# A convolution block moved from VectorE to ScalarE and GpSimd, and a swap and a load moved ahead, in the first steps of a fused convolution and GELU MLP

## The chip, the cores and the metric

The kernel runs on 1 core of one Trainium2 chip. Times are device microseconds of one execution of the program. An engine is TensorE (PE; its weight loads are PEld), VectorE (DVE), ScalarE (ACT), GpSimd (POOL) or SyncE (SP, which here only issues DMAs). PSUM is the memory that TensorE writes, SBUF the one that all engines share.

## The reference

x has shape (8, 4096, 192) and goes through two blocks. The first is a causal convolution along the sequence, with 7 taps per head, softmaxed; 8 heads share the 192 channels. The second takes each of the 32768 tokens through two products with a quick GELU between them. All is float32.

```python
w = softmax(weight)                       # (8 heads, 7 taps)
x_pad = concat([zeros(B, 6, D), x], axis=1)
out[b, s, h, g] = sum_k w[h, k] * x_pad[b, s + k, h, g]
h = out.reshape(32768, 192) @ w_in        # (192, 2048)
g = h * (1 / (1 + exp(-1.702 * h)))
y = g @ w_out                             # (2048, 192)
```

## The kernel before, in words

The 32768 tokens are cut into 32 steps. A step (`big` in the code) takes 512 tokens from each of two halves of the batch. Channels lie on partitions; the 192 channels are three chunks `c` of 64, and a chunk's 512 tokens lie as two halves of 256 on the two halves of the partitions. A block of the convolution is named by its number: chunk c, batch half n is block 2c + n.

A step has two parts on TensorE. The first product is `hidden`: w_in times the convolved x. It runs a list written out by hand, `HIDDEN`, of 40 terms and the instructions between them. Each term is one product of a sum of weight blocks with a sum of convolution blocks (a fast matrix multiplication: fewer products, more sums). The sums of weight blocks are `SUMS_W`, made once, in steps 0 and 1. The sums of convolution blocks are made anew in every step (blocks 6 to 19). VectorE joins the products (`join`), ScalarE copies them out of PSUM and computes the GELU into the buffer `g`. The second product is `second`, with a hand-written list `PLAN`: w_out times g, again with sums. The weight forms of this product are `w_form`.

While step s is in these two parts, step s+1's convolution blocks are summed and step s+2's x is transposed and convolved. What step s+1 needs:

- The x of a step is loaded by `load_x` (L87, DMAs at L99, 8 of them on SP's queue) into `xin`, of which there is one buffer, and turned by three transposes on VectorE (`transpose_x`, L518) into `xts`, of which there is one buffer too.
- The taps. From step 3 on, all three chunks are convolved by ScalarE taps (`tap`, L570: one tap times x, into a free half of some block of `g` or `room`) and added by GpSimd, VectorE and accumulating DMAs. For step 2 only chunks 0 and 2 go this way, and the adding is by accumulating DMAs on GpSimd's queue (`end_taps`, L600). They form a tree: for the homes of taps 1 to 6 and the result 0, first (1,2), (3,4), (5,6), then (0,1), (3,5), and (0,3) last. Chunk 1 of step 2 is convolved on VectorE: seven instructions in `conv` (L551 once, L553 six times), from the generator `prepare`.
- The sums of blocks (`sum_of`, L604, printed as L435 and L437 inside `add_up`) and the swap of a block (`cross_run`, L609: two DMAs on SP's queue that bring each half of the partitions to the other, since a term wants both halves on each).

In step 1 the sums and swaps for step 2 are held back until the third `("turn",)` in `HIDDEN`. At that point the list calls `need("done 2")`, which issues the last two accumulating DMAs of chunk 2, and then GpSimd makes two sums for block 12 (`over`, L870) and five others, and SP swaps them as they come. `("fetch",)`, the fourth term from the end of the list's 41 products, is step 2's first term and reads block 12.

Step 0 is written out (`first_step`); its second product is `second_first` (L922), in which `go` runs the products (L980) and pops one entry of the list `side` beside each (L985). At its end, and in step 1's first product, runs everything that is done once: 24 sums of weight blocks on VectorE for one half of w_in and 18 for the other (`sums_w_in`, L445), block 13's sum and swap, the last four forms of w_out (`add_forms(3)`: four ScalarE copies and four accumulating DMAs, L482), the turns and stores of step 0's output (L1091, L1102), and the load of x for step 3. The pieces that go beside the list are in `beside`: from the second join on, each join takes one entry off it (L819).

In the listing, the lines that the change touches are L685 (`prepare`), L818 (`join`), L845 (`turn`), L913 (the end of `hidden`), L1002 to L1074 (`second_first`), and L1078 (`convs_next`).

Of the kernel before, what the change touches and what calls it, by code (L numbers as in the profile page):

```python
# [15 lines left out]
def kernel(  # L16
# [29 lines left out]
    nc = tc.nc  # L46

    B, S, D = x.shape
    H, K = weight.shape
# [5 lines left out]
    NC = D // R  # L55
# [25 lines left out]
    vec, act = nc.vector, nc.scalar  # L81
# [5 lines left out]
    def load_x(big, ns=range(2)):  # L87


        p, c = divmod(big, CHUNKS)  # L90
        if c == 0 and 0 in ns:
            (nc.gpsimd if big else vec).memset(xin[0:R, :, 0, :], 0.0)
        for n in ns:
            for o in range(2):
                j = 1 if c == 0 and o == 0 else 0
                t = c * TOK + o * T + (j - 1) * Q
                for v in range(2):
                    q0 = o * R + v * Q
                    nc.sync.dma_start(  # L99
                        out=xin[q0 : q0 + Q, n, j:NJ, :],  # L100
                        in_=x_v[n, p, t : t + (NJ - j) * Q, v * Q : v * Q + XW].rearrange(
                            "(j i) d -> i j d", i=Q
                        ),
                    )
# [33 lines left out]
    def spot(i):  # L138

        if i >= SPOTS:  # L140
            return block(*divmod(i - SPOTS, NG))
        flat = osbs[:, i * BLK : (i + 1) * BLK] if i < 2 else room[:, ROOMS[i - 2], :]
        return flat.rearrange("p (k t) -> p k t", k=NG)
# [55 lines left out]
    def own(big):  # L199
        return conv_t[:, big % 2 * NR : big % 2 * NR + NR, :]  # L200
# [13 lines left out]
    SUMS_ES = [  # L214
        (13, 0, "-", 3), (14, 1, "-", 3), (15, 1, "-", 11),
    ]
# [228 lines left out]
    def sums_w_in(v, n0=0, n1=None):  # L445
        for item in SUMS_W[v][n0:n1]:
            add_up(lambda j: w_in_s[:, j, v * P : (v + 1) * P], *item)
# [63 lines left out]
    cw = consts.tile([P, NC, K], F32)  # L511
# [31 lines left out]
    def conv_src(big, c, k, ns=slice(0, 2)):  # L543
        return xts[big][:, c, ns, Q - PAD + k : Q - PAD + k + T]
# [57 lines left out]
    def sum_of(big, item, eng=None):  # L602

        add_up(lambda i: pair(big, i)[:, 0, :], *item, eng=eng or nc.gpsimd)  # L604
# [8 lines left out]
    def cross_run(big, b0, b1, eng=None):  # L613

        (o, x), n = places_of(big, b0), b1 - b0
        cross(conv_t[:, x : x + n, :], conv_t[:, o : o + n, :], eng)
# [7 lines left out]
    V_E = (V_F[1], V_F[1] + NV_E)  # L624
# [59 lines left out]

    def prepare(big):  # L685

        if big < 3:
            for k in range(K):
                yield "", 0.76 if k else 0.48, lambda k=k: conv(big, 1, k)
        yield f"conv {big}", 0.0, lambda: None  # L690
        if big == 1:
            dst = own(1)[:, 0:2, :]
            for k in (1, 3, 5):
                yield "", 0.7, lambda k=k: vec.tensor_add(dst, dst, tap_home(1, 0, k))
        yield f"done {big}", 0.0, lambda: (need(f"taps {big}"), end_taps())
# [71 lines left out]
    FETCH, NEXT = (1, 0), (3, 1, 2, 0)  # L767
# [7 lines left out]
    def hidden(big, tiles, work):  # L775
# [34 lines left out]
        def join(dst, a, op, b):  # L810
            flat = "o" not in (dst[0], a[0], b[0])
            if dst[0] == a[0] == b[0] == "k":
                banks = [[KS[int(n[1:])] for n in (dst, a, b)]]
            else:
                banks = [[bank(n, h) if flat else ot(bank(n, h)) for n in (dst, a, b)] for h in range(2)]
            for out, x, y in banks:
                (vec.tensor_add if op == "+" else vec.tensor_sub)(out, x, y)  # L817
            seen_joins.append(0)  # L818
            if beside and len(seen_joins) > 1:  # L819
                beside.pop(0)()  # L820

        def gelu(i, src, sign):
            dst = g_rows(i)
# [13 lines left out]
        def next_turn():  # L837
            c = next(turns)
            if c == 0:
                need(f"done {big + 1}")  # L840
            transpose_x(big + 2, c)
            if c == NC - 1 and big + 3 < N_BIG:
                load_x(big + 3)

        def turn():  # L845
            seen.append(0)
            if big > 1:
                if big + 2 < N_BIG:
                    next_turn()
            elif len(seen) == 1:  # L850
                add_forms(3)
            elif len(seen) == NC:
                while beside:
                    beside.pop(0)()
                next_turn()
                need("forms")
                held.clear()
                while waiting:
                    waiting.pop(0)()
# [52 lines left out]
        )  # L912
        for item in HIDDEN:  # L913
            do[item[0]](*item[1:])
        if big == 1:
            for _ in range(1, NC):
                next_turn()

    def chunk_cols(c):
        return slice(c * Q, (c + 1) * Q)  # L920
# [1 line left out]
    def second_first(between, fetch, last_taps):  # L922
# [40 lines left out]
        def listed(w, t, gs=(0, 1)):  # L963
            return [
                (w[i][:, v, h, :], t[i][:, v, :, h * T : (h + 1) * T])
                for i in gs for v in range(2) for h in range(2)
            ]
# [9 lines left out]
        def go(bank, steps, first=True, more=False):  # L977
            for i, (w, t) in enumerate(steps):
                for c in range(NC):
                    nc.tensor.matmul(  # L980
                        chunk(bank, c), w[:, chunk_cols(c)], t,
                        start=first and i == 0, stop=not more and i == len(steps) - 1, skip_group_check=True,
                    )
                dst, w, t, start, to = side.pop(0)
                nc.tensor.matmul(dst, w, t, start=start, stop=to is not False, skip_group_check=True)  # L985
                if to is not False:
                    act.copy(to, dst)
# [3 lines left out]
        def sums_b(i):  # L991
# [10 lines left out]
        p2, p3 = listed(a12, b21), listed(s4, b22)  # L1002
        aside(
            (sums[0], sums[1], c11),
            (listed(s1, t1, (0,)), None, True), (listed(s1, t1, (1,)), p5, False), (p3[:6], q12, False),
        )
        last_taps()
        add_forms(0)
        sub(t1[1], b12[1], b11[1])
# [24 lines left out]
        act.copy(whole(c21), whole(a))  # L1034
        add(p5, p5, whole(a))
        go(c12, p3[6:], first=False)
        sums_w_in(FETCH[0], 0, 3)
        sums_w_in(1 - FETCH[0], 0, 24)
        next_tap()
# [7 lines left out]
        fetch()  # L1047
        act.copy(last, whole(c21))
        add(q12, q12, whole(c12))
        sum_of(1, SUMS_ES[0], vec)  # L1050
        cross_run(1, V_E[0], V_E[0] + 1)
        sums_w_in(1 - FETCH[0], 24)

        def after_1():
# [7 lines left out]
        def beside_1():  # L1062
            turn(0, 0, blocks(p1), js)
            for item in SUMS_ES[1:]:
                sum_of(1, item, vec)
            cross_run(1, V_E[0] + 1, V_S[1])
            store(0, 0)
            load_x(3)

        after_copy.extend([after_1, after_2])  # L1070
        beside.append(beside_1)
        for i in range(3, len(SUMS_W[FETCH[0]]), 6):
            beside.append(lambda i=i: sums_w_in(FETCH[0], i, i + 6))
        beside.extend([lambda: convs_next(1)] * K)  # L1074

    after_copy, beside = [], []

    def convs_next(n):  # L1078
        for _ in range(n):
            if todo and not todo[0][0]:  # L1080
                todo.pop(0)[2]()

    def blocks(t):
        return t.rearrange("p (j t) -> p j t", t=Q)
# [387 lines left out]
```

## Time and profile before

| | us |
|---|---|
| median of 3 runs | 2269.74 |
| lowest and highest run | 2267.92, 2270.87 |
| the profiled execution | 2267.85 |
| its span (first to last instruction) | 2266.1 |
| PE busy | 2251.1 (99%) |
| DVE busy | 2114.3 (93%) |
| ACT busy | 1710.6 (75%) |
| POOL busy | 985.0 (43%) |

The profile is of one execution. Each row of a timeline gives start and length in us, engine, line, operation, out<-in and shapes, then in brackets the idle time of the engine before it and what ended it. Instructions of one kind in a row are merged, with their count (x8). A group row gives the count, the busy time in us and the mean of one in ns, then the idle time before them. A DMA's row gives the time of its issue; when its data has landed is a number of its own. L12 is line 12 of the kernel.

### The profile page before, as it was taken

The numbers are of one execution on the slowest core, as the hardware profiler recorded it, in microseconds if no ns is written. First come the engines' busy times: TensorE is split into PE (matmuls) and PEld (weight loads), VectorE is DVE, ScalarE is ACT, GpSimd is POOL, SyncE is SP. The second block draws the span as 40 slices with busy tenths as digits, with TensorE's granted clock in tenths as the row PEclk, the third lists the DMA queues.
The fourth block names the chain that finished last, engine by engine and source line by source line (L and its number), as shares of the span: only waits on it lengthen the run. The fifth ranks groups of instructions, "written<-read, shape, count | busy, mean of one in ns | idle before, by whom it ended". The sixth has DMA issues, their size and how long they took to land.

```text
span 2266.1 us, 63896 instructions
## 1 busy us (share of the span) xinstructions
PE 2251.1 (99%) x25090; PEld 1345.5 (59%) x25090; DVE 2114.3 (93%) x3268; ACT 1710.6 (75%) x3335; POOL 985.0 (43%) x1009
## 2 busy tenths in 40 slices
PE   9999999999999999999999999999999999999999
PEld 5356656666556666566665566665666656666555
DVE  8999999999999999999999999999999999999998
ACT  8767777777877777777778777787777877777854
POOL 1534554444543445434445435454344454344510
PEclk9999999999999999999999999999999999999999
DMA  9986778767688767787676886677876768765743
GB/s 204 160 169 141 143 143 168 150 134 146 136 159 164 142 138 143 146 169 145 138 147 134 161 162 140 137 143 148 169 143 138 147 136 165 157 137 112 138 95 71
DMA packets 341995, 329.66 MB, mean 145 GB/s; under 512 B 131648, under 2 KB 280768, under 8 KB 341696
## 3 DMA queue, kind: packets, MB, share of 16 engines
q0 software_dynamic: 66352, 167.47, 41.9%
q1 hardware_dynamic: 273696, 157.72, 30.4%
q8 instruction: 199, 3.26, 0.6%
q14 instruction: 100, 0.82, 0.1%
q10 hardware_dynamic: 1648, 0.39, 0.1%
HBM read 53.15 MB, written 25.17 MB: 35 GB/s over the span
## 4 chain that ended last, share of the span: by engine, by line
PE 96%; issue 1%; DMA 1%; SPq 1%; DVE 1%; ACT 0%; POOL 0%; DVEq 0%; POOLq 0%; ACTq 0%
PE slot L709 37%; PE slot L1172 28%; PE sums L1172 17%; PE sums L709 13%; PE slot L980 2%; DMA xin<-in_x_dram 0%; SPq L99 0%; DMA osbs<-room 0%; SPq L1102 0%; POOL conv_t L437 0%; DVE xt L518 0%; DVE g L435 0%; ACT conv_t L1278 0%; DVE conv_t L437 0%; POOL g L1148 0%
## 5 line engine op out<-in xcount | busy, mean ns | idle before, releaser
L709 PE MATMUL slot<-conv_t,w_in_s 64*128 64x512 f32 x3372 | 823.6, 593 | 3.5 <-ACT slot L802 2.4
L1172 PE MATMUL slot<-g,w_form 128*32 128x256 f32 x5872 | 713.4, 379 | 0.8 <-ACT slot L1201 0.8
L709 PEld LDWEIGHTS slot<-conv_t,w_in_s 64*128 64x128 f32 x3372 | 449.8, 187 | 287.9 <-issue 175.0
L437 DVE TENSOR_TENSOR g<-g 128x1024 f32<-128x1024 f32 x372 | 443.5, 1219 | 10.8 <-ACT g L833 1.9
L1172 PE MATMUL sums<-g,w_form 128*32 128x256 f32 x3800 | 422.2, 379 | 0.0
L1172 PEld LDWEIGHTS slot<-g,w_form 128*32 128x32 f32 x5872 | 364.1, 110 | 90.9 <-ACT slot L1201 1.2
L826 ACT ACTIVATE g<-slot 128x512 f32<-128x512 f32 x494 | 265.1, 625 | 132.0 <-PE slot L709 131.4
L709 PE MATMUL sums<-conv_t,w_in_s 64*128 64x512 f32 x1284 | 346.7, 592 | 0.9 <-DMA conv_t<-conv_t 0.6
L1172 PE MATMUL slot<-g,w_out_s 128*32 128x256 f32 x4080 | 321.4, 379 | 0.9 <-DVE g L437 0.5
L1148 POOL DMA_DIRECT2D g<-g x124 | 116.5, 939 | 450.5 <-PE slot L1172 252.4
L1197 ACT COPY room<-slot 32x256 f32<-32x256 f32 x434 | 158.4, 365 | 186.7 <-PE slot L1172 172.8
L570 ACT ACTIVATE g<-xt,cw 128x512 f32<-128x512 f32 x389 | 270.2, 719 | 4.4
L437 POOL TENSOR_TENSOR conv_t<-conv_t 128x256 f32<-128x256 f32 x210 | 195.4, 948 | 152.4 <-PE slot L709 90.3
L1172 PEld LDWEIGHTS sums<-g,w_form 128*32 128x32 f32 x3800 | 211.0, 110 | 69.6
L1172 PEld LDWEIGHTS slot<-g,w_out_s 128*32 128x32 f32 x4080 | 166.0, 110 | 127.0 <-ACT g L826 11.4
L906 POOL TENSOR_TENSOR conv_t<-conv_t,g 128x512 f32<-128x512 f32 x174 | 238.6, 1393 | 4.5
L709 PEld LDWEIGHTS sums<-conv_t,w_in_s 64*128 64x128 f32 x1284 | 171.1, 187 | 106.2 <-issue 56.2
L833 ACT ACTIVATE g<-g 128x1024 f32<-128x1024 f32 x155 | 170.7, 1101 | 1.5 <-DVE g L817 1.5
L906 POOL TENSOR_TENSOR g<-g 128x512 f32<-128x512 f32 x87 | 110.7, 1273 | 121.9 <-ACT g L570 119.6
L1197 ACT COPY room<-sums 32x256 f32<-32x256 f32 x217 | 79.3, 366 | 104.7 <-PE sums L1172 92.2
L709 PE MATMUL slot<-g,w_in_s 64*128 64x512 f32 x556 | 149.7, 593 | 1.7 <-DVE slot L817 1.7
L826 ACT ACTIVATE g<-sums 128x512 f32<-128x512 f32 x188 | 103.8, 615 | 58.6 <-PE sums L709 58.1
(243 smaller groups left out, 3901.7 us busy)
## 6 DMA issues: line engine op xcount, KB each, us to landing
g<-g POOLq DMA_DIRECT2D x124, 512.0 KB, 6.6
conv_t<-conv_t SPq DMA_DIRECT2D x844, 64.0 KB, 2.0
xin<-in_x_dram SPq DMA_DIRECT2D x240, 180.0 KB, 6.3
out_dram<-osbs SPq DMA_DIRECT2D x186, 128.0 KB, 2.5
g<-g POOLq DMA_DIRECT2D x66, 256.0 KB, 6.5
g<-g SPq DMA_DIRECT2D x248, 64.0 KB, 3.6
g<-room POOLq DMA_DIRECT2D x31, 512.0 KB, 6.1
g<-osbs POOLq DMA_DIRECT2D x30, 512.0 KB, 6.5
```

Of the source, the lines that this page charges most:

```text
L437: eng.tensor_sub(v(dst), v(a), v(b))
L570: act.mul(home, conv_src(big, c, k), cw[:, c, k : k + 1])
L709: nc.tensor.matmul(slot[h], w_in_s[halves[h], a, v * P : (v + 1) * P], src, start=first, stop=True, skip_group_check=True,)
L826: act.activation(dst[:, :, h, :], ot(bank(src, h)), AF.Gelu_apprx_sigmoid, scale=float(sign))
L833: act.activation(dst.rearrange("p o h t -> p h o t"), src, AF.Gelu_apprx_sigmoid, scale=float(sign))
L906: (vec if eng == "v" else nc.gpsimd).tensor_add(dst, dst, home)
L980: nc.tensor.matmul(chunk(bank, c), w[:, chunk_cols(c)], t, start=first and i == 0, stop=not more and i == len(steps) - 1, skip_group_check ...
L1148: nc.gpsimd.dma_start(out=spot(dst), in_=spot(a), accum_op=ALU.add)
L1172: nc.tensor.matmul(dst, w, t, start=first, stop=last, skip_group_check=True)
L1197: act.copy(to, d)
```

## The change

Five things are changed.

- Chunk 1 of step 2 is no longer convolved by VectorE (`prepare` starts at step 2 without it). Its seven taps become ScalarE taps, and six GpSimd adds in their new function `middle_tap`, each add right behind its tap in the program's order. The homes of taps 1 to 6 are halves of spots 11, 12, 15, 3, 3 and 11; taps 1 and 2 lie where the GELU of output block 5 is to be written, tap 3 where that of block 9 is, tap 6 where that of block 7 is.
- The 18 weight sums that remain go two to each of nine joins, with a tap beside each of the first seven; before, they went six to each of three joins, with a convolution instruction to each of the next seven.
- Block 13's sum and swap, and the load of x for step 3, go out in `second_first` before the last 24 weight sums, ahead of step 0's stores on SP's queue. Before, the sum and swap came after the last product of step 0 and the load after the first joins of step 1 and the stores.
- So that the swap can go there, the last 18 entries of `side` are reordered: the steps that read the memory of block 13's swap come first, and the three column chunks alternate.
- Step 3's transposes go out at the twelfth join, the third turn and the thirteenth join; before, one at the third turn and two after the list. With the last of them goes the load of x for step 4.

```diff
@@ -684,7 +684,7 @@
-        if big < 3:
+        if big < 2:
             for k in range(K):
                 yield "", 0.76 if k else 0.48, lambda k=k: conv(big, 1, k)
         yield f"conv {big}", 0.0, lambda: None
@@ -817,7 +817,7 @@
             seen_joins.append(0)
             if beside and len(seen_joins) > 1:
-                beside.pop(0)()
+                (beside.pop(0) or next_turn)()
@@ -850,7 +850,7 @@
             elif len(seen) == NC:
-                while beside:
+                while beside and beside[0]:
                     beside.pop(0)()
                 next_turn()
                 need("forms")
@@ -912,9 +912,7 @@
         for item in HIDDEN:
             do[item[0]](*item[1:])
-        if big == 1:
-            for _ in range(1, NC):
-                next_turn()
+        assert not beside
@@ -1002,8 +1000,10 @@
         aside(
             (sums[0], sums[1], c11),
-            (listed(s1, t1, (0,)), None, True), (listed(s1, t1, (1,)), p5, False), (p3[:6], q12, False),
+            (listed(s1, t1, (0,)), None, True), (listed(s1, t1, (1,)), p5, False), (p3[4:6] + p3[:4], q12, False),
         )
+        tail = side[-18:]
+        side[-18:] = [tail[6 * c + i] for i in range(6) for c in range(NC)]
         last_taps()
@@ -1034,6 +1034,9 @@
         go(c12, p3[6:], first=False)
+        sum_of(1, SUMS_ES[0], vec)
+        cross_run(1, V_E[0], V_E[0] + 1)
+        load_x(3)
         sums_w_in(FETCH[0], 0, 3)
         sums_w_in(1 - FETCH[0], 0, 24)
         next_tap()
@@ -1047,8 +1050,6 @@
         act.copy(last, whole(c21))
         add(q12, q12, whole(c12))
-        sum_of(1, SUMS_ES[0], vec)
-        cross_run(1, V_E[0], V_E[0] + 1)
         sums_w_in(1 - FETCH[0], 24)
@@ -1065,20 +1066,28 @@
             cross_run(1, V_E[0] + 1, V_S[1])
             store(0, 0)
-            load_x(3)
 
         after_copy.extend([after_1, after_2])
         beside.append(beside_1)
-        for i in range(3, len(SUMS_W[FETCH[0]]), 6):
-            beside.append(lambda i=i: sums_w_in(FETCH[0], i, i + 6))
-        beside.extend([lambda: convs_next(1)] * K)
+        n = len(SUMS_W[FETCH[0]])
+        for j in range(max(K, (n - 2) // 2)):
+            def more(j=j):
+                sums_w_in(FETCH[0], 3 + 2 * j, 5 + 2 * j)
+                if j < K:
+                    middle_tap(j)
+            beside.append(more)
+        beside.extend([None] * 2)
 
     after_copy, beside = [], []
-
-    def convs_next(n):
-        for _ in range(n):
-            if todo and not todo[0][0]:
-                todo.pop(0)[2]()
+    MIDDLE = ((11, 0), (12, 0), (15, 0), (3, 0), (3, 2), (11, 2))
+
+    def middle_tap(k):
+        dst = own(2)[:, 2:4, :]
+        s, h = MIDDLE[k - 1]
+        home = spot(s)[:, h : h + 2, :] if k else dst
+        act.mul(home, conv_src(2, 1, k), cw[:, 1, k : k + 1])
+        if k:
+            nc.gpsimd.tensor_add(dst, dst, home)
```

## The prediction

> **What bounds the kernel now.** I read the page first, then the table by stage (columns: stretch, its length, busy us and instructions of PE, PEld, DVE, ACT and POOL, granted clock, DMA share, GB/s). The change touches what is issued at the end of step 0 and in the first product of step 1, so I cut there: first product of step 1, second product of step 1, and the same two of step 2, which the change leaves alone.
>
> ```profile
> span 2266.1 us, 63896 instructions
> ```
> ```profile
> 92.16:141.74 49.58, 43.98 (x173) 24.63 (x169) 45.77 (x85) 34.34 (x65) 19.77 (x21) 0.97 0.82 150
> 141.74:177.92 36.18, 34.50 (x627) 19.92 (x626) 33.31 (x52) 24.73 (x52) 11.20 (x13) 1.00 0.99 200
> 177.92:213.55 35.63, 35.63 (x168) 21.98 (x172) 33.93 (x51) 28.40 (x53) 20.68 (x19) 1.00 0.55 122
> 213.55:247.36 33.81, 33.81 (x627) 20.20 (x626) 31.19 (x49) 25.03 (x53) 11.27 (x13) 1.00 0.96 179
> ```
>
> Step 2 runs at TensorE's own pace: its two parts take 35.63 and 33.81 us, with PE busy all the time. Step 1 takes 49.58 and 36.18. So all that can be won is 13.95 + 2.37 = 16.3 us, 0.7% of the span, and only in step 1. Next I read VectorE's order of work through the first product.
>
> ```profile
> 94.92 1.28 DVE L804 COPY g<-slot 128x512 f32<-128x512 f32 x2
> ...
> 100.33 1.29 DVE L804 COPY room<-slot 128x512 f32<-128x512 f32 x2 [1.14 <-PE slot L709]
> ...
> 114.28 0.48 DVE L551 TENSOR_SCALAR conv_t<-xt,cw 128x512 f32<-128x512 f32 x1
> ...
> 120.87 1.23 DVE L437 TENSOR_TENSOR g<-g 128x1024 f32<-128x1024 f32 x1 [0.53 <-ACT g L833]
> ...
> 129.51 0.78 DVE L518 STREAM_TRANSPOSE xt<-xin 128x576 f32<-128x576 f32 x1 [1.83 <-DMA xin<-in_x_dram]
> ...
> 138.71 1.27 DVE L817 TENSOR_TENSOR g<-room,slot 128x512 f32<-128x512 f32 x2
> ...
> 143.31 1.42 DVE L518 STREAM_TRANSPOSE xt<-xin 128x576 f32<-128x576 f32 x2
> ```
>
> From the first copy (94.92) to the end of the last join (139.98) VectorE idles 1.14 + 0.53 + 1.83 = 3.5 us in 45.1. It bounds the part. But a second chain ends at almost the same time, on GpSimd's queue (POOL).
>
> ```profile
> 97.82 0.86 POOL L600 DMA_DIRECT2D g<-g  x1 [2.19 <-DMA g<-g]
> 102.96 0.86 POOL L600 DMA_DIRECT2D conv_t<-g  x1 [4.28 <-DMA g<-g]
> 103.50 2.97 POOL L600 DMA_DIRECT2D g<-g  x3
> 109.73 0.86 POOL L600 DMA_DIRECT2D conv_t<-g  x1 [3.27 <-DMA g<-g]
> 110.27 2.09 POOL L482 DMA_DIRECT2D w_form<-w_out_s  x2
> 111.34 2.78 POOL L482 DMA_DIRECT2D w_out_s<-w_form  x2
> 113.24 1.76 POOL L600 DMA_DIRECT2D g<-g  x1
> 123.81 0.86 POOL L600 DMA_DIRECT2D conv_t<-g  x1 [8.81 <-DMA xin<-in_x_dram]
> 130.11 0.72 POOL L435 TENSOR_TENSOR conv_t<-conv_t 128x256 f32<-128x256 f32 x1 [5.44 <-PE slot L709]
> ```
>
> These are the accumulating DMAs that add up the taps of step 2's blocks 0 and 2. The last two, at 113.24 and 123.81, depend on each other. The view of that source line, cut to one issue, gives the time to landing of those at 97.82, 113.24 and 123.81, in this order:
>
> ```profile
> DMA to landing us min/median/max: 4.6/4.6/4.6
> ```
> ```profile
> DMA to landing us min/median/max: 10.3/10.3/10.3
> ```
> ```profile
> DMA to landing us min/median/max: 6.2/6.2/6.2
> ```
>
> So the last lands at 123.81 + 6.2 = 130.0, and at 130.11 POOL begins the sums of step 2's blocks (the releaser named there had long been done). The first pair of sums makes block 12, which the fetch of step 2 needs; the fetch is the fourth term from the end of the first product, and TensorE takes its terms in order.
>
> **The change, part by part.**
>
> ```profile
> L553 DVE SCALAR_TENSOR_TENSOR conv_t<-xt,cw,conv_t 128x512 f32<-128x512 f32 x6 | 4.5, 746 | 0.0
> ...
> L817 DVE TENSOR_TENSOR slot<-g,osbs 128x512 f32<-128x512 f32 x2 | 2.3, 1217 | 0.0
> ...
> L817 DVE TENSOR_TENSOR slot<-room,osbs 128x512 f32<-128x512 f32 x2 | 1.3, 694 | 0.0
> ```
>
> VectorE loses the seven convolution instructions: 4.5 us and 0.48 us of busy time; an instruction overlaps the next by some 0.1 (two joins of 694 ns are busy for 1.3 us), so 4.4 us of the queue. It gains two of the three transposes of step 3, which today run at 143.31, after the part: 1.4 us. The weight sums stay the same 18, spread. Block 13's sum and swap go out before the 24 weight sums: the swap lands about 5 us earlier, and the wait of 1.14 us goes. The load of x for step 3 goes out some 20 us earlier, and the wait of 1.83 us goes. The reordered side products of step 0 are the same count; I cost them at nothing, since the three copies behind them run beside the weight sums (bounds 0 and one 0.6 us copy).
>
> VectorE alone would then end its joins 3.5 + 4.4 - 1.4 = 6.5 us sooner.
>
> ScalarE gets seven taps, POOL six adds, and SP's queue a new order:
>
> ```profile
> L570 ACT ACTIVATE g<-xt,cw 128x512 f32<-128x512 f32 x389 | 270.2, 719 | 4.4
> ...
> L906 POOL TENSOR_TENSOR conv_t<-conv_t,g 128x512 f32<-128x512 f32 x174 | 238.6, 1393 | 4.5
> ...
> conv_t<-conv_t SPq DMA_DIRECT2D x844, 64.0 KB, 2.0
> ```
> ```profile
> 83.75 6.45 SPq L609 DMA_DIRECT2D g<-g  x7
> ...
> 112.07 10.41 SPq L99 DMA_DIRECT2D xin<-in_x_dram  x8
> 132.52 13.07 SPq L609 DMA_DIRECT2D conv_t<-conv_t  x20
> 145.69 4.04 SPq L99 DMA_DIRECT2D xin<-in_x_dram  x8
> ```
>
> The taps are 7 x 0.72 = 5.0 us on ScalarE, which idles 49.58 - 34.34 = 15.2 us in the part: covered, and up to 2 us late where the part gets dense (two copies there also wait for stores that SP now issues behind the load). The six adds are the point. POOL works in order, and its queue stands still in the waits for DMA landings shown above. The first add sits behind the DMA of 102.96, the other five behind the four of L482; the last two accumulating DMAs come behind all six. Two gelu of ScalarE write where taps 1, 2 and 3 lie and wait for adds 2 and 3.
>
> The load of x, at about 91.6 (SP is free at 90.2, then the swap), now meets the DMAs of block 0. What two queues do to each other is seen today at 118 to 121 us, where POOL's accumulating DMAs and the load run together:
>
> ```profile
> q0 software_dynamic: 319, 0.46, 89.7%
> q1 hardware_dynamic: 299, 0.18, 24.7%
> ```
>
> The load takes a fourth, so POOL's DMAs are stretched a little: I take the issue of 102.96 at 104.5 (between 103 and 107). Then:
>
> - add 1 behind it, 1.4 us: the next three DMAs at 104.5 + 0.5 + 1.4 = 106.4 instead of 103.5;
> - from there to the place of today's 113.24 it is 9.7 us as now: add 2 starts at 116.1;
> - five adds of 1.4: 123.1, where the last but one DMA is issued, 9.9 us later than now;
> - it no longer meets the load, so it lands after 4.6 instead of 10.3: 127.7; the last is issued at 128.0 and takes 4.7: 132.7, that is 2.7 later than today's 130.0;
> - two sums 2.4 (130.11 to 132.52 today), the second half of the swap 0.5 later, landing 2.0: the fetch starts at 137.6;
> - four terms to the end.
>
> ```profile
> 93.29 0.86 PE sums L709 x4
> ```
>
> At 0.86 a term the first product ends at 141.0, against 141.74: 0.7 us won of the 6.5. With t0 at 103 and adds of 1.27 it would be some 3 us, with t0 at 107 and landings of 6.2 some 5 us lost.
>
> In the second product of step 1 today's excess of 2.37 us goes with one DMA: the same kind, a step later, is much quicker.
>
> ```profile
> DMA to landing us min/median/max: 9.4/9.4/9.4
> ```
> ```profile
> DMA to landing us min/median/max: 6.1/6.1/6.1
> ```
>
> (osbs<-room at 155.2, and at 225.5.) It runs beside the load for step 4, issued at 145.69 behind 20 swaps. After the change that load goes out behind 18 swaps that begin at 135.1: at about 147, so the meeting stays. VectorE enters that part without its two transposes. Bounds: 2.4 won, 1.5 lost; I take 0.5 won, near nothing, because the load stays there.
>
> Sum: 0.7 + 0.5 = 1.2 us won. Against the profiled execution (2267.85 us, of which 2266.1 are the span) that is 2266.7; the median shown is 2269.74, so the forecast is **2268.6 us**.
>
> **The rivals.**
>
> - B, POOL's chain does not bind: the landings are short and the adds slip into the waits, and VectorE's 6.5 us come through, with 1 us in the second product: 2269.74 - 7.5 = 2262.2. For it: VectorE is the one that idles least now, and four of POOL's DMAs are quicker without the load beside them. Against it: the addition above leaves only 0.7, and five adds stand ahead of a chain of two landings.
> - C, slower: the adds and VectorE block each other. While POOL added blocks at 131 to 138, VectorE's joins with both operands in SBUF took 1217 ns instead of 694 (rows above), and POOL's own adds stretched from 0.72 us (row of 130.11) to
>
> ```profile
> L437 POOL TENSOR_TENSOR conv_t<-conv_t 128x256 f32<-128x256 f32 x6 | 7.3, 1253 | 0.1
> ```
>
>  Stretched like that, an add of 1.39 takes 2.4, six of them 6 us more; the last landing is at 138.7, the part ends 5.3 later than today, and the sum is 2274.5. It decides from adds of about 1.7 us on, where the gain is gone. Against it: in the new place the joins around the adds mostly read PSUM, and only the short weight sums and two or three joins read SBUF twice. The Trainium skill, "SBUF — State Buffer", section "Who interferes with whom", states that a VectorE instruction with two SBUF inputs and a GpSimd instruction that reads SBUF lock each other out for whole instructions. The rows of 131 to 138 agree with it (1217 against 694 ns); by that rule the weight sums beside the adds would each cost an add their full length.
> - D, it does not do what it says: the swap and the load, issued earlier, land no earlier, because the DMA engines are full from 92 on. Then the fall is VectorE's only and POOL's chain is as in the forecast: within 2 us of it, and counted there.
>
> **How the numbers follow.** Forecast with D 0.50, its own range 2265 to 2273; B 0.30; C 0.20. The range that should hold it 8 times in 10 takes half of B and most of C: 2262 to 2275. A measurement of this kernel can tell about 0.2%, 4.5 us, from no change. Faster by more: B and the low end of the forecast, 0.32. Slower by more: C, 0.21. Within: 0.47.
>
> **What would show it.** In the new profile the seven L551 and L553 instructions are gone from VectorE between 92 and 142, and its waits for xin and at 100 us with them. POOL shows five adds in a row and behind them the last two L600 DMAs at about 123 and 128, each landing in under 5 us; the first block sum starts at 132 to 133. The first product is 48 to 50 us long and PE waits just before its last four terms, for a swap. I am wrong towards B if the last L600 DMA is issued before 125 or the fetch does not wait; wrong towards C if the adds take 2 us or more; and wrong on the second product if the osbs<-room DMA lands in 6 us.

## The result: slower by 0.27%, and the profile after

The changed kernel takes 2274.93 us (median of 9 runs, 2273.05 to 2276.79), the kernel before 2268.65 us in the same job (9 runs, 2267.46 to 2270.87). The ratio is 1.0027, its 95% interval 1.0016 to 1.0037: slower by 6.3 us, just inside the range, on the side that had a chance of 0.21. Where kernels below come from other jobs, they are compared with the kernel before in their own job. The runs of E6, E10 and E13 lie in two groups some 4 us apart, so the medians of these three are less sharp than the others.

The span of the profiled execution, from the page of after:

```profile
span 2272.5 us, 63912 instructions
```

The table by stage of after (columns as in the prediction: stretch, length, busy us of PE, PEld, DVE, ACT and POOL, granted clock, DMA share, GB/s). The first two rows lie in step 0; the last two are the two products of step 1.

```profile
79.10:84.50 5.40, 0.00 (x0) 0.00 (x0) 5.40 (x8) 4.65 (x6) 0.69 (x1) 0.74 1.13 186
84.50:88.00 3.50, 3.50 (x20) 0.87 (x24) 1.96 (x3) 0.00 (x0) 0.88 (x2) 0.50 0.69 138
100.33:145.78 45.45, 43.47 (x169) 22.36 (x168) 42.96 (x72) 38.40 (x72) 26.92 (x26) 1.00 0.70 130
145.78:183.24 37.46, 34.80 (x626) 20.01 (x625) 32.28 (x50) 24.73 (x52) 11.20 (x13) 1.00 0.96 198
```

Step 1 begins at 100.33 instead of 92.16: 8.2 us are lost at the end of step 0, where the prediction put the reordered side products at nothing. The first product is then shorter (45.45 against 49.58 us), the second longer (37.46 against 36.18), and step 2 begins at 183.24 instead of 177.92, 5.3 us late. In step 0 TensorE does nothing for 5.4 us, and the clock granted over the next 3.5 us is 0.50 of full speed. Before, the same stretch had no gap:

```profile
56.00:92.16 36.16, 36.16 (x336) 10.62 (x336) 35.57 (x62) 27.19 (x49) 22.25 (x25) 1.00 0.95 157
```

TensorE's timeline of after names what ended the gap, and VectorE's timeline shows why that came late:

```profile
78.05 1.04 PE L978 MATMUL slot<-g,conv_t 128*32 128x512 f32 x6
84.50 1.06 PE L983 MATMUL slot<-g,conv_t 128*32 128x512 f32 x1 [5.42 <-DVE conv_t L1030]
```
```profile
78.03 2.28 DVE L1027 TENSOR_TENSOR osbs<-g,osbs 128x2048 f32<-128x2048 f32 x1
80.23 2.29 DVE L1028 TENSOR_TENSOR room<-g,room 128x2048 f32<-128x2048 f32 x1
82.43 1.43 DVE L437 TENSOR_TENSOR g<-conv_t 128x256 f32<-128x256 f32 x4
83.77 0.68 DVE L1030 TENSOR_TENSOR conv_t<-conv_t,slot 96x512 f32<-96x512 f32 x1
```

L983 is a product of `side`. In the new order the first entry for column chunk 2 is the third of the last 18, and it goes to c11, one of the banks that PSUM is divided into. VectorE's add `add(p1, p1, whole(c11))` (L1030) still has to read that bank, and it stands behind two subtractions of 2.3 us and four sums. Before, chunk 2's entries were the last six, long after that add.

GpSimd's queue, VectorE beside it, the osbs<-room DMA of the second product, and TensorE at the fetch, in after:

```profile
120.32 4.65 POOL L1090 TENSOR_TENSOR conv_t<-conv_t,g 128x512 f32<-128x512 f32 x2
125.05 2.95 POOL L1090 TENSOR_TENSOR conv_t<-conv_t,room 128x512 f32<-128x512 f32 x2
128.08 2.34 POOL L1090 TENSOR_TENSOR conv_t<-conv_t,g 128x512 f32<-128x512 f32 x1
130.37 0.87 POOL L600 DMA_DIRECT2D g<-g  x1
133.95 0.86 POOL L600 DMA_DIRECT2D conv_t<-g  x1 [2.71 <-DMA g<-g]
137.39 0.72 POOL L435 TENSOR_TENSOR conv_t<-conv_t 128x256 f32<-128x256 f32 x1 [2.58 <-DMA conv_t<-g]
```
```profile
122.32 3.21 DVE L817 TENSOR_TENSOR sums<-osbs,g 128x512 f32<-128x512 f32 x2 [0.88 <-ACT g L826]
125.45 2.71 DVE L435 TENSOR_TENSOR w_in_s<-w_in_s 128x128 f32<-128x128 f32 x2
```
```profile
DMA to landing us min/median/max: 10.9/10.9/10.9
```
```profile
141.60 1.22 PE L709 MATMUL slot<-conv_t,w_in_s 64*128 64x512 f32 x4 [0.21 <-DMA conv_t<-conv_t]
```

Five adds in a row and the two landings behind them stand as forecast, but the five take 130.37 - 120.32 = 10.05 us, 2.0 each instead of 1.4, and two joins on VectorE take 3.21 us instead of 1.3. The wait for the swap before the last four terms, forecast as a sign, is 0.21 us here: TensorE came to it 8.2 us late, and GpSimd's chain lost less than that. Probably for the same reason the first product is 45.45 us long and not the 48 to 50 of the forecast.

### The profile page after: what moved, and what is told of

The parts are those of the page before. It is cut to its first block, busy times and chain, and to the rows that moved or that the text cites. A ratio compares the mean times of both kernels' runs of the same rounds, so it can differ in the third digit from the quotient of the medians.

```text
span 2272.5 us, 63912 instructions
## 1 busy us (share of the span) xinstructions
PE 2254.4 (99%) x25090; PEld 1342.9 (59%) x25090; DVE 2112.8 (93%) x3261; ACT 1714.4 (75%) x3342; POOL 992.9 (44%) x1015
## 4 chain that ended last, share of the span: by engine, by line
PE 93%; DVE 3%; DMA 2%; issue 1%; POOL 1%; SPq 0%; ACT 0%; POOLq 0%; DVEq 0%; ACTq 0%
PE slot L709 35%; PE slot L1181 28%; PE sums L1181 17%; PE sums L709 12%; DMA g<-g 1%; DMA g<-in_moe_w_in_dram 1%; PE sums L983 0%; DMA g<-osbs 0%; SPq L340 0%; DMA conv_t<-conv_t 0%; PE slot L983 0%; DVE w_out_s L420 0%; POOL conv_t L1090 0%; DVE g L437 0%; DVE g L990 0%
## 5 line engine op out<-in xcount | busy, mean ns | idle before, releaser
L437 DVE TENSOR_TENSOR g<-g 128x1024 f32<-128x1024 f32 x372 | 443.5, 1219 | 10.9 <-DMA g<-osbs 2.3
L826 ACT ACTIVATE g<-slot 128x512 f32<-128x512 f32 x494 | 265.1, 625 | 127.4 <-PE slot L709 126.5
```

Of the source, the lines that this page charges most:

```text
L437: eng.tensor_sub(v(dst), v(a), v(b))
L826: act.activation(dst[:, :, h, :], ot(bank(src, h)), AF.Gelu_apprx_sigmoid, scale=float(sign))
```

## The experiments

Two theories stood against each other at first: **the side order** (the loss is the wait for the bank c11) and **the taps and adds** (rival C: GpSimd's adds cost by themselves). E1 to E4 ran in one job (before 2269.25 us), E6 to E9 in a second (2269.65), E10 to E13 in a third (2268.87).

**E2: the kernel before with the side order alone**

```diff
-            (listed(s1, t1, (0,)), None, True), (listed(s1, t1, (1,)), p5, False), (p3[:6], q12, False),
+            (listed(s1, t1, (0,)), None, True), (listed(s1, t1, (1,)), p5, False), (p3[4:6] + p3[:4], q12, False),
+        tail = side[-18:]
+        side[-18:] = [tail[6 * c + i] for i in range(6) for c in range(NC)]
```

> The kernel before the change, with the reordered side products alone. Theory 1: the loss is all here: the same wait of 5 to 6 us on L1030 at about 79 us, and 6 to 8 us slower than before, 2275 to 2277 us. Theory 2: the order is free, 2268 to 2270 us.

2273.71 us, ratio 1.0020 (1.0011 to 1.0029). TensorE's longest wait:

```profile
PE slot L985 <- DVE conv_t L1032: 5.6, 1, 5.6
```

The reorder alone makes the wait and loses 4.5 us. Step 1 begins at 100.58, and some of the 8.4 us come back in step 1 (its products take 48.68 and 34.41 us).

**E3: the changed kernel with the bank's add moved up**

```diff
         make_common_1()
+        add(p1, p1, whole(c11))
         sub(t2[1], b21[1], t2[1])
         sub(t2[0], b21[0], t2[0])
         make_late_1()
-        add(p1, p1, whole(c11))
```

> The kernel after the change with one line moved: VectorE's add of p1 (L1030, the reader of the bank) is issued before the two big subtractions and the four late sums, so at about 78 instead of 84 us. The reordered side products stay. Theory 1: the wait falls under 1 us and the time is 2274.9 less 7 to 8, 2266 to 2268 us. Theory 2: 2274 to 2275 us.

2271.90 us, ratio 1.0009 (1.0000 to 1.0017). TensorE has no wait in step 0 any more, and step 1 begins at 92.44. So the side order cost some 3.6 us of the 6.3 (2.65 us over before are left), and something else costs the rest. Without the delay, this kernel shows the chain that the prediction added up. GpSimd's timeline of E3, then two rows of TensorE's, then the stage:

```profile
116.28 5.54 POOL L1090 TENSOR_TENSOR conv_t<-conv_t,g 128x512 f32<-128x512 f32 x2
...
125.85 0.87 POOL L600 DMA_DIRECT2D g<-g  x1
129.44 0.86 POOL L600 DMA_DIRECT2D conv_t<-g  x1 [2.72 <-DMA g<-g]
```
```profile
122.50 6.31 PE L709 MATMUL slot<-conv_t,w_in_s 64*128 64x512 f32 x19 [1.91 <-ACT g L826]
```
```profile
138.31 2.17 PE L709 MATMUL slot<-conv_t,w_in_s 64*128 64x512 f32 x4 [3.48 <-DMA conv_t<-conv_t]
```
```profile
140.00:145.00 5.00, 5.00 (x14) 2.30 (x10) 1.94 (x3) 2.17 (x4) 2.45 (x2) 0.56 0.44 107
```

The fetch starts at 138.31, after a wait of 3.48 us for the swap. It and the three terms behind it take 6.7 us, at a clock of 0.56 over the last 5 us, where the prediction has 3.4. An earlier wait, 1.91 us at 122.50 for a GELU, also has a stretch at half clock behind it, from 124.0 to 127.4; what held the GELU is seen in E6.

**E1 and E7: the end of step 0 as before, the rest changed**

E1 takes only the reorder out of the changed kernel:

```diff
-            (listed(s1, t1, (0,)), None, True), (listed(s1, t1, (1,)), p5, False), (p3[4:6] + p3[:4], q12, False),
+            (listed(s1, t1, (0,)), None, True), (listed(s1, t1, (1,)), p5, False), (p3[:6], q12, False),
-        tail = side[-18:]
-        side[-18:] = [tail[6 * c + i] for i in range(6) for c in range(NC)]
```

> The kernel after the change, with the side products of step 0's last 18 entries in the order of before; all else of the change stays. Theory 1 (the reordered side products stall TensorE: the third one goes into the bank that VectorE's late add at L1030 reads, 5.4 us, and TensorE runs at half clock for some 4 us behind it, 8.2 us in all): the stall is gone, the first product of step 1 starts at 92 instead of 100 us, and the time is about 2267 to 2269 us (the swap of block 13 has to wait for the end of the side products again, so its 1 to 1.5 us come back). Theory 2 (GpSimd's adds and VectorE lock each other, rival C of the prediction): nothing changes, 2274 to 2275 us.

2276.22 us, ratio 1.0030 (1.0020 to 1.0041). It isn't a clean test, and the expectation had the order of two instructions wrong: block 13's swap stands ahead of the last side products in the program, so these read what the swap has written (that part of the result is changed) and wait for it, 7.4 us in TensorE's waits:

```profile
PE sums L983 <- DMA conv_t<-conv_t: 7.4, 1, 7.4
```

E7 therefore puts block 13's sum and swap back behind the last product as well, but leaves the early load of x:

```diff
-        sum_of(1, SUMS_ES[0], vec)
-        cross_run(1, V_E[0], V_E[0] + 1)
         load_x(3)
...
         add(q12, q12, whole(c12))
+        sum_of(1, SUMS_ES[0], vec)
+        cross_run(1, V_E[0], V_E[0] + 1)
```

> The changed kernel with the end of step 0 as before in one point: the side products in their old order, and block 13's sum and swap behind the last product, where they were. The taps, the adds, the spread weight sums, the early load of x and the earlier transposes stay. Theory 'two costs' (the side order costs by its wait for a bank, the taps and adds cost by themselves): no wait of TensorE in step 0, a wait of VectorE of 1 to 1.5 us for the swap at the start of step 1, and a time of 2270.5-2273, close to the 2271.9 of E3. Rival 'the early swap earns what the rest loses': without it 2274 or more. Rival 'all of the loss is the side order': 2266-2268.

2275.20 us, ratio 1.0026 (1.0016 to 1.0036): the time that the rival "the early swap earns what the rest loses" gave, but for a reason that none of the three theories had. SP's queue, then TensorE:

```profile
89.82 8.74 SPq L99 DMA_DIRECT2D xin<-in_x_dram  x8
98.67 1.65 SPq L609 DMA_DIRECT2D conv_t<-conv_t  x2
```
```profile
105.93 3.57 PE L709 MATMUL slot<-conv_t,w_in_s 64*128 64x512 f32 x8 [8.50 <-DMA conv_t<-conv_t]
```

Now the swap is queued behind the eight DMAs of the load, and TensorE waits 8.50 us for it. By E1 and E7 the load may go out early only behind an early swap, and the early swap needs the new side order: three parts of the change hang together, and the reorder can't just be undone.

**E4: E3 with VectorE's convolution kept**

```diff
-        if big < 2:
+        if big < 3:
...
-                    middle_tap(j)
+                    convs_next(1)
```

> As the kernel with the add moved up, and chunk 1 of step 2 is convolved by VectorE again (seven instructions beside the same joins), so no middle taps and no GpSimd adds. Theory 1 with the prediction's account of step 1: VectorE's 4.4 us come back and GpSimd's queue loses 8 us; the first product of step 1 is 47 to 48 us, 1 to 3 us slower than with the adds, 2267 to 2270 us. Theory 2 (the adds cost the time): 5 us and more faster than the kernel with the add moved up.

2266.08 us, ratio 0.9985 (0.9976 to 0.9994): faster than before, 5.8 us under E3. The taps and adds cost that much, although VectorE has seven instructions less in E3. The two kernels' joins and weight sums at the same place, E3 and then E4:

```profile
114.95 3.14 DVE L817 TENSOR_TENSOR sums<-osbs,g 128x512 f32<-128x512 f32 x2 [0.47 <-ACT g L826]
118.01 1.55 DVE L435 TENSOR_TENSOR w_in_s<-w_in_s 128x128 f32<-128x128 f32 x2
```
```profile
118.23 1.29 DVE L817 TENSOR_TENSOR sums<-osbs,g 128x512 f32<-128x512 f32 x2
119.43 0.60 DVE L435 TENSOR_TENSOR w_in_s<-w_in_s 128x128 f32<-128x128 f32 x2
```

VectorE starts these joins 3.3 us earlier in E3 and ends its last join of the list (136.10 + 1.27 = 137.37 in E3, 136.31 + 1.27 = 137.58 in E4) at the same time: it has won nothing. Two sub-theories for the 5.8 us: **order** (the adds stand ahead of the chain of two landings) and **lock** (the adds and VectorE's instructions with two SBUF inputs hold each other up).

**E6: E3 with the last two landings between the adds**

```diff
     def middle_tap(k):
...
+        if k == 2:
+            end_taps(1)
         if k:
             nc.gpsimd.tensor_add(dst, dst, home)
+        if k == 5:
+            end_taps()
```

> E3 (the add on bank c11 moved up) with one more edit: the last two accumulating DMAs of chunk 2 no longer wait behind all six adds of chunk 1. The last but one, (3,5), is issued behind the second add and the last, (0,3), behind the fifth, so that the adds pass while it travels. Theory 'order' (the adds cost because they stand ahead of a chain of two landings): the last landing comes some 4 to 5 us sooner than the 132.76 us of E3, at 127 to 129, the fetch does not wait 3.48 us, and the time falls from 2271.9 to 2266-2268. Theory 'lock' (the adds cost because they and VectorE's instructions with two SBUF inputs hold each other up): VectorE's stretched sums (3.14 us for two joins, 1.55 for two short sums) are still there and VectorE ends its joins no sooner than in E3 (137.4), so the time stays at 2269.5-2271.5 even where the wait for the swap is gone.

2268.97 us, ratio 0.9999 (0.9990 to 1.0008). The fetch no longer waits: the order cost 3.3 us (2.65 over before in E3, 0.7 under it here). What is left is the wait for a GELU that E3 had too, now 3.13 us long. GpSimd, ScalarE, TensorE and the stage of E6:

```profile
117.97 5.43 POOL L1092 TENSOR_TENSOR conv_t<-conv_t,g 128x512 f32<-128x512 f32 x2
```
```profile
122.02 1.08 ACT L826 ACTIVATE g<-slot 128x512 f32<-128x512 f32 x2 [2.40 <-POOL conv_t L1092]
```
```profile
124.08 6.31 PE L709 MATMUL slot<-conv_t,w_in_s 64*128 64x512 f32 x19 [3.13 <-ACT g L826]
```
```profile
124.00:128.00 4.00, 3.92 (x11) 2.19 (x13) 3.96 (x6) 4.00 (x9) 3.92 (x4) 0.68 0.16 28
```

ScalarE waits to write a GELU where tap 2 lies, until GpSimd has added it; TensorE waits for the GELU to free its bank.

**E8: E3 with the weight sums six to a join**

```diff
-                sums_w_in(FETCH[0], 3 + 2 * j, 5 + 2 * j)
+                sums_w_in(FETCH[0], 3 + 6 * j, 9 + 6 * j)
```

> E3 with one part of the change undone: the 18 weight sums go six to each of the first three of those joins again; the taps and adds stay one to a join. The weight sums (two SBUF inputs) then lie ahead of most of the adds instead of beside them. Theory 'lock': the adds behind the third join have less to meet, VectorE's sums are back near 0.6 us for a pair, the last landing comes 2 to 4 us before the 132.76 of E3, and the time is 2268-2270. Theory 'order': the adds are as long and the landings come as in E3; the taps go out later behind longer joins, and the time is 2271-2274.

2271.97 us, ratio 1.0008 (0.9999 to 1.0017): as E3. The lock is still there, with other partners. VectorE's joins and one large sum, and GpSimd's adds beside them:

```profile
116.21 2.53 DVE L817 TENSOR_TENSOR slot<-room,osbs 128x512 f32<-128x512 f32 x2
118.66 3.43 DVE L817 TENSOR_TENSOR sums<-osbs,g 128x512 f32<-128x512 f32 x2
122.00 2.29 DVE L437 TENSOR_TENSOR g<-g 128x1024 f32<-128x1024 f32 x1
```
```profile
116.32 5.21 POOL L1090 TENSOR_TENSOR conv_t<-conv_t,g 128x512 f32<-128x512 f32 x2
```

The lock theory's own expectation, shorter adds, fell: with the weight sums gone from there, the joins and the large sum take their place. Where the weight sums lie makes no difference.

**E12: E6 without the six adds**

```diff
         if k:
-            nc.gpsimd.tensor_add(dst, dst, home)
+            pass
```

> E6 with the six GpSimd adds of chunk 1 left out: ScalarE makes the seven taps as in the change, and block 1 holds the first tap alone. It prices all six adds at once, their lock with VectorE, their hold on the GELUs and their place in GpSimd's queue. Theory 'the adds alone cost, the taps are covered': VectorE has lost its convolution and meets no adds, so its joins end 3 to 4.4 us sooner than E4's 137.6 unless TensorE or a landing binds first, the first product is 44 to 46 us, and the time is 2263-2266. Rival 'the taps cost too' (ScalarE is late with its copies and GELUs): the first product stays at 47 us or more and the time at 2266.5 or more.

2265.87 us, ratio 0.9985 (0.9977 to 0.9994). This is the most telling run. VectorE has lost its convolution and meets no adds, and still the first product takes 46.26 us, exactly as in E4, which convolves on VectorE. The stretch from 107.4 to 130 in E4 and in E12 (ACT's busy time is the fourth of the five):

```profile
107.40:130.00 22.60, 20.56 (x80) 11.55 (x77) 22.53 (x46) 19.64 (x37) 10.96 (x13) 1.00 0.84 151
```
```profile
107.40:130.00 22.60, 19.99 (x78) 9.61 (x76) 18.55 (x39) 21.56 (x40) 11.33 (x13) 1.00 0.85 152
```

In E4 VectorE is busy for 22.53 of 22.60 us and ScalarE idles 2.96. In E12 VectorE idles 4.05 and ScalarE 1.04: the taps have filled ScalarE, and VectorE waits for its GELUs:

```profile
120.27 1.23 DVE L437 TENSOR_TENSOR g<-g 128x1024 f32<-128x1024 f32 x1 [1.91 <-ACT g L833]
```

The work has only moved from one full engine to the next. The adds' part is seen in the same run: without them, the pair of joins that took 3.14 us in E3 takes 1.30:

```profile
116.54 1.30 DVE L817 TENSOR_TENSOR sums<-osbs,g 128x512 f32<-128x512 f32 x2 [0.70 <-ACT g L826]
```

This is neither theory in full: the time lies within 2263 to 2266, but the joins end no sooner than in E4.

**E10: E6 with adds 2 and 3 reading their own block**

```diff
-            nc.gpsimd.tensor_add(dst, dst, home)
+            nc.gpsimd.tensor_add(dst, dst, dst if k in (2, 3) else home)
```

> E6 (landings between the adds), but the adds of taps 2 and 3 read block 1 itself in place of the taps' homes, so what block 1 sums up to is changed; the number of adds, their shapes and their places stay. In E6 TensorE waits 3.13 us at 124.1 for a GELU that is to be written into tap 2's home and waits until GpSimd has added that home, in an add stretched to 4.03 us. Theory 'homes' (what is left of the cost after E6 is this hold on the GELU): no such wait of TensorE, the first product is 2 to 3 us shorter than E6's 48.5, and the time is 2265-2267 against 2268.97. Rival 'lock' (VectorE itself is late, by its joins and sums held up beside the adds): the wait changes its name, VectorE's joins end where they did in E6 (139.4), and the time is 2268-2269.5.

2266.64 us, ratio 0.9994 (0.9985 to 1.0002), 1.5 us better against before than E6, which is less than the two intervals can tell apart. The long wait is gone and shorter ones of other names have come, in TensorE's timeline; the stage shows half clock behind these too:

```profile
127.93 0.69 PE L709 MATMUL sums<-conv_t,w_in_s 64*128 64x512 f32 x1 [0.79 <-DVE sums L817]
...
131.59 2.65 PE L709 MATMUL slot<-g,w_in_s 64*128 64x512 f32 x4 [0.82 <-DVE slot L817]
```
```profile
132.00:136.00 4.00, 3.99 (x9) 1.94 (x9) 4.00 (x6) 1.19 (x2) 4.00 (x5) 0.67 0.42 100
```

This one is inconclusive. The median lies where the theory of the homes has it; by the profiles the first product fell only from 48.54 to 48.16 us, as the lock would have it. How the 2.3 us of the adds (E6 against E12) divide between hold and lock stays open.

**E11: the moves alone**

The kernel before with E2's reorder, E3's moved add, and

```diff
         go(c12, p3[6:], first=False)
+        sum_of(1, SUMS_ES[0], vec)
+        cross_run(1, V_E[0], V_E[0] + 1)
+        load_x(3)
```

(and these three lines taken from where they stood.)

> The kernel before with the moves alone: side products reordered and the bank's add moved up, block 13's sum and swap and the load of x for step 3 sent out before the last weight sums. VectorE convolves chunk 1 as before, weight sums six to a join, step 3's transposes one at the third turn and two after the list. Theory 'the moves earn it': the waits of VectorE of 1.14 and 1.83 us are gone, the last accumulating DMA of chunk 2 lands 2 to 4 us earlier than 130.0, and the time is 2265.5-2267.5, near E4's 2266.08. Rival 'the order of sums and transposes earns it': 2268-2269.5, near the kernel before.

2265.52 us, ratio 0.9983 (0.9974 to 0.9992): 3.35 us won, as much as E4 with its spread sums and earlier transposes (3.2). The moves of swap and load, with the order and the add that they need, are what earns in this change, and VectorE's two waits are gone. What these cost in before is more than their length. There a join stood behind the transpose that waited 1.83 us for x, TensorE waited for that join, and ran at half clock behind it (before: a row of TensorE's, then the stage):

```profile
133.10 2.35 PE L709 MATMUL slot<-g,w_in_s 64*128 64x512 f32 x3 [1.75 <-DVE slot L817]
```
```profile
132.00:136.00 4.00, 2.90 (x6) 1.72 (x8) 4.00 (x5) 0.60 (x1) 4.00 (x5) 0.68 0.27 66
```

The profile of E11 shows full clock in all of step 1 and a first product of 45.44 us instead of 49.58. Its second product is longer, 37.37 us, for the reason that E9 shows.

**E9 and E13: the load for step 4 earlier**

E9 is E4, E13 is E6, each with:

```diff
                 held.clear()
+                waiting.pop(0)()
+                while beside:
+                    beside.pop(0)
+                    next_turn()
                 while waiting:
                     waiting.pop(0)()
```

> E4 (chunk 1 of step 2 kept on VectorE, the bank's add moved up) with one more edit: the rest of step 3's transposes, and with the last of them the load of x for step 4, go out at the third turn right behind the first of the held sums and its swap, not at the next join. In E4 the load went out at 142.7 and met the osbs<-room DMA of the second product. Theory 'meeting' (that DMA takes 9 to 11 us because it runs beside this load): the load goes out at 134 to 137, the DMA lands in 6 to 8 us, the second product takes 34.3-35.3 us instead of 36.1, and the time is 2264.5-2265.8 against 2266.1. Rival: VectorE's two transposes, moved ahead of the last joins, cost the first product as much as the second wins, and the time is 2266-2267.5.

2263.99 us, ratio 0.9975 (0.9965 to 0.9984), **the quickest kernel of this study**, 5.7 us under before. The load goes out at 131.1 instead of 142.7, and the second product, in E4 and in E9:

```profile
139.22:175.32 36.10, 34.23 (x626) 20.05 (x625) 32.37 (x50) 24.74 (x52) 11.20 (x13) 1.00 1.00 202
```
```profile
138.95:173.16 34.21, 34.02 (x625) 20.08 (x624) 32.27 (x50) 24.75 (x52) 11.20 (x13) 1.00 0.95 182
```

The osbs<-room DMA there, E4 and E9:

```profile
DMA to landing us min/median/max: 10.6/10.6/10.6
```
```profile
DMA to landing us min/median/max: 8.7/8.7/8.7
```

The second product is 1.9 us shorter; the DMA lands 1.9 sooner, though not in the 6 to 8 us expected, and VectorE's wait for it is gone. Over all fourteen profiles the trend is the same: where the load goes out 6.5 to 8.8 us ahead of this DMA, it takes 10.5 to 11.1 us; at 9.3 to 10.4 ahead, 7.6 to 10.1; at 20 and more (E9, E13), 8.7 and 7.7.

> E6 with the edit of E9: the change with its taps and adds kept and its three costs answered as far as they can be (the bank's add moved up, the landings between the adds, the rest of step 3's transposes and the load of x for step 4 right behind the first held swap). If the second product's gain of E9 is independent of the taps: 2266.5-2267.5, some 2 us below E6 and some 3 us above E9, which convolves on VectorE. If the transposes, ahead of VectorE's last joins, cost as much as they win beside adds and sums on GpSimd: 2268.5-2270.

2266.28 us, ratio 0.9991 (0.9982 to 1.0000). The second product falls to 33.81 us, so the gain doesn't hang on the taps. The kernel with all parts of the change, mended, is 2.6 us under before and 3.1 us behind E9, which leaves the taps and adds out.

## Why the prediction was wrong

Against before, in each one's own job, the loss comes apart as follows; the last column is the difference of two neighbours.

| kernel | against before, us | what this step prices |
|---|---|---|
| E11, the moves alone | -3.35 | the moves: 3.35 won |
| E12, taps, no adds | -3.0 | taps for VectorE's convolution, spread sums, earlier transposes: nothing won |
| E6, landings between the adds | -0.7 | six adds, lock and hold: 2.3 lost |
| E3, landings behind the adds | +2.65 | the order, and the half clock after it: 3.3 lost |
| after | +6.3 | the side order's wait: 3.6 lost |

Each number against before has an interval of some 2 us to either side, so a difference of two has some 3. The order and the side order (3.3 and 3.6) are just clear of that; the 2.3 us of the adds are not.

The clock is part of these prices. In steps 0 and 1 the profiles show stretches at a clock of 0.50 that last 3.5 or 7 us: one of 3.5 in before, none in E4, E9, E11 and E12, one of 3.5 in E6, one of 3.5 and one of 7 in E3, one of 7 in after. A stretch of 3.5 us in which TensorE works all the time costs some 1.7 us (half of it, an estimate). So by these profiles about half of what the moves won, and most of what the adds lost, went through the clock. One profile of each kernel doesn't show that its other runs have the same stretches.

- **The side products, "I cost them at nothing" (bounds 0 and one 0.6 us copy): failed.** I looked at the copies behind the products and not at the bank that each is written to and at who still had to read it. It cost 5.42 us of waiting and the half clock behind it (0.50 over 3.5 us), 8.2 us at the start of step 1, of which 3.6 last. Without it (E3) the kernel is still not faster than before, so it is not the whole error of the sign.
- **"VectorE alone would then end its joins 6.5 us sooner": failed.** The waits and the convolution are gone as counted. But E12 shows that the joins do not come sooner when VectorE is free: ScalarE paces them. Of the 4.05 us that VectorE idles in the stretch, it waits 2.6 for ScalarE and 1.4 for TensorE, which itself waited 1.06 for a copy of ScalarE. I had covered the taps by 15.2 us of idle time of ScalarE in the whole part; in the stretch where they lie it has 3 us for 5 us of taps. So rival B, at 0.30, had no ground here: its 6.5 us were not there to be had.
- **The chain on GpSimd: right in its end, by two errors that cancel.** The last landing was forecast at 132.7, and E3 has it at 132.8. The five adds start at 116.28 (116.1 forecast) and take 9.6 us instead of 7.0, and each landing takes 3.3 us instead of 4.6 and 4.7.
- **"Four terms to the end" at 0.86: failed.** After its 3.48 us of waiting TensorE took 6.7 us for them, at 0.56 of the clock. The first product ends at 145.0 in E3, not at 141.0. This alone turns the forecast gain of 0.7 into a loss. The table that the prediction starts from had a sign of it: a clock of 0.97 in the first product of before, which is the stretch at half clock shown under E11, and which the sum leaves out. In after itself the term was not at work, since the 8.2 us lost earlier had hidden the wait for the swap.
- **Rival C was right in kind and had too little weight.** It was to decide from adds of 1.7 us; they take 2.0 in after and 1.9 in E3. What spoke against it, that the joins there mostly read PSUM, is true, but the few that read SBUF twice were enough: `sums<-osbs,g` is caught in after and E3, `slot<-room,osbs` in E8. The weight sums, on which the prediction put the price of the lock, don't set it (E8).
- **The hold on the GELUs** was named, and priced as covered. It shows as a wait of TensorE of 1.91 us in E3 and of 3.13 in E6, where ScalarE waits 2.40.
- **The second product, "0.5 won": wrong by 1.8** (37.46 against 36.18 us). The osbs<-room DMA took 10.9 us, where it took 9.4 before. The mechanism named there, the meeting with the load, is right, and E9 removes it; its size had the wrong sign. The prediction's own times (the load at 147, the first product's end at 141.0) put the load 6.0 us into the second product instead of 3.95, which means a closer meeting. It went out 5.8 us into it (151.55 against 145.78), 6.5 us ahead of the DMA instead of 9.5.

## What to carry over

Before products are reordered, list for each the bank that it writes and the last reader of that bank, with that reader's place in its own engine's queue; a free buffer is a property of the order. Idle time that is to cover moved work must be read from the stretch where the work lands: E4's ScalarE idles 3 us of the 22.6 where the taps come. And a wait of TensorE can cost more than its length: look for stretches of half clock behind waits, in the kernel before as well. Here one stood behind a wait of 1.75 us (before), and none behind one of 1.28 (E4).

## What the runs showed of the hardware

- **The clock after a wait.** Granted clock 0.50 over the 3.5 us after a wait of 5.42 us (after), 0.56 over 5 us after one of 3.48 us (E3), 0.68 over 4 us after one of 3.13 us (E6), and 0.68 over the 4 us around one of 1.75 us (before). In E10 it is 0.67 over 4 us in which TensorE was busy for 3.99, behind two waits of 0.8 us. All these stretches last about 3.5 or 7 us, and while TensorE waits long, a part of them passes in the wait. The Trainium skill, "TensorE: Matmul & The Clock Gate", section "What's actually happening", has the clock halve after an idle window of about 3.4 us, in windows that run freely. The lengths agree with such a window; the cause doesn't: in the 3.4 us ahead of the drop TensorE was idle for 1.7 us in before and 0.8 in E10. What decides below 3.4 us, no run here shows.
- **The lock is mutual and finds other partners.** A pair of joins with both operands in SBUF goes from 1.29 to 3.14 us (E4, E3) beside adds of 1.3 to 3 us, and is back at 1.30 without the adds (E12). The Trainium skill, "SBUF — State Buffer", section "Who interferes with whom", says that they lock each other out; the rows agree, and E8 shows that clearing one kind of instruction out of the way doesn't help when the next in the queue is of the same kind.
- **The wait for the bank.** The add reads 96 partitions of it, the side product writes the other 32 (its copy, L985, is 32 x 512). The Trainium skill, "PSUM — Partial Sum Buffer", section "PSUM bank collisions raise a hardware error", states that different quadrants of one bank may be accessed at once, by which this wait would not be needed. No run here took it away, so that stays open; E3 avoids it by order alone.
- **An accumulating DMA that meets nothing** lands in 3.3 us (E3 and E6, at 129 and 126), where the kernel before has 4.6 to 10.3. In the 3.2 us behind these two issues no other DMA shows.
